# Low parts cut into two or three GpSimd operations, a smaller decode credit in the attention stage, and a last store moved into a branch

## The chip, the cores and the metric

One core of a Trainium2 chip runs the whole program: TensorE (PE) multiplies, VectorE (DVE), ScalarE (ACT) and GpSimd (POOL) do the element work, SyncE (SP) issues nearly all transfers. The metric is device time in microseconds, as the median of several runs.

## The reference

Windowed attention with a linear position bias, then two feed-forward blocks, all on 2 x 768 tokens of width 512:

```python
scores = scale * np.matmul(q, k.transpose(0, 1, 3, 2)) + bias      # 8 heads of 64
a = softmax(where(is_global | is_local, scores, -1e9))             # first 8 keys, last 96 keys
x = a @ v
h = x^T @ U @ V;  u = x + h^T                                      # rank 32, over the tokens
x = u + np.maximum(u @ w_ch1, 0.0) @ w_ch2                         # 512 -> 2048 -> 512
h = np.maximum(x @ w_in, 0.0);  u, v = halves of h                 # 512 -> 2 x 512
v_n = layer norm of v
v_s = np.einsum('ts,bsd->btd', w_spatial, v_n) + b_spatial
out = (u * v_s) @ w_out
```

U, V, w_ch1, w_ch2, w_in and w_out arrive as 64-bit floats; n_global and n_local are data.

## The kernel before

Each large product is done in split precision: an operand a is held as a high part h (a rounded, type fp32r) and a low part l = a - h, and `gemm` (L275 to L277) issues three matmuls per term, h by h, l by h and h by l. Low parts come from `sub` (L58), a subtraction on POOL in most places.

**Weights.** The class `Weights` streams 28 pieces of 128x1024 (six of them 128x768). A coded piece arrives as two halves r (L156, SP). Decoding a half takes an absolute value on ACT (L69) and four DVE operations: clamp (L74), shift (L75) and two joins (L81, L84), each of 128x512. When both halves are done, ACT writes the piece's high part h (L206) and POOL its low part l (L58). A ring holds five pieces. The calls `step(time)` set the pace: each adds a credit, each decode operation spends some. In the attention stage `step(DECODE[0])` is called in four of every six steps after step 24 (the constants MIXING and START); later `step(DECODE[1])` is called once per group of matmuls. The order in which these calls are written is the order on the engines; every engine works through its queue in that order.

**Attention stage** (to about 110 us). Eight head pairs of six query tiles, one step a tile. For each tile PE makes scores sc (L692), DVE adds the bias and takes the row maximum (s and m, L703), ACT exponentiates (e, L706), PE transposes (pt, L716), ACT or DVE copies (et, L63 or L65), PE multiplies by v (xp), DVE normalises every three tiles into x (L755 to L757). There are three banks for sc: PE can start the next scores only when DVE has read the ones two tiles before. After six tiles `mix` adds the rank-32 term: ACT writes xh (L300), POOL xl, PE forms T (L312; ACT L316 and DVE L318 evict it) and u (L291, L295; ACT L339 evicts it), ACT writes uh (L342) and POOL ul. For the last pair DVE makes xl itself.

**Feed-forward stage.** `run` walks four groups g of the hidden width: first products c of token chunk 0 and 1, second product y of chunk 0, then c 2, y 1, y 2. Pieces 0 and 1 are the first products' weights of group 0, pieces 2 and 3 its second products' weights. ACT and DVE evict c (L357, L358), DVE adds y to u (L405). In the rest of the run come the layer norm, the spatial product with gate gs, gh, gl, and twelve output tiles: the last one in two halves, each evicted by ACT (L519) and stored by SP (L520).

**End.** A flag computed on DVE says whether n_local or n_global are out of the windows' reach; each engine loads it (L927) and branches (L928) past a general path that is not taken here.

Of the kernel before, what the change touches and what calls it, by code (L numbers as in the profile page):

```python
# [9 lines left out]
F32 = mybir.dt.float32  # L10
# [7 lines left out]
B, H, S, D = 2, 8, 768, 64  # L18
P = 128
NT = S // P  # L20
DM = H * D
# [27 lines left out]

START, DECODE, MIXING = 24, (1.1, 1.5), (1, 4)
UVSTART = 3
SLOPES = [2.0 ** (-(h + 1)) for h in range(H)]


def sub(eng, out, a, hi):
    eng.tensor_tensor(out=out, in0=a, in1=hi.bitcast(F32), op=ALU.subtract)  # L58


def copy(nc, eng, out, in_):
# [48 lines left out]
class Weights:  # L110
# [86 lines left out]
    def emit(self):  # L197

        nc = self.nc
        for p, (_, _, a, n) in enumerate(self.order):  # L200
            while p >= self.decoded or p - RING >= self.freed:
                yield
            hi = self.ring.tile([P, a, n], F32R, name=f"h{p}", tag="whi")
            lo = self.ring.tile([P, a, n], F32R, name=f"l{p}", tag="wlo")
            wv = self.w32.pop(p)[:, :a * n].rearrange("p (a n) -> p a n", a=a)
            nc.scalar.activation(out=hi, in_=wv, func=AF.Copy)  # L206
            sub(nc.gpsimd, lo, wv, hi)
            self.ready.append((hi, lo))
            yield

# [21 lines left out]
class Moe:  # L232


    def __init__(self, tc, ctx, consts, w, out, ps, pfx):
        self.nc = tc.nc
        self.tc = tc
        self.c = consts
        self.w = w
        self.out = out  # L240
        self.ps = ps
        self.two = self.rest = None
        self.only_scores = False
        self.pfx = pfx
        pool = lambda n, b: ctx.enter_context(tc.tile_pool(name=pfx + n, bufs=b))
        self.act = pool("act", 1)
        self.q = pool("q", 2)
        self.u32 = self.wide("u32")
# [30 lines left out]
    def mix(self, pool, x, b, d, u, last=False):  # L279

        nc, c = self.nc, self.c
        eng = nc.vector if last else nc.gpsimd
        bank = lambda tag: self.two.tile([P, 512], F32, name=self.pfx + "up", tag=tag, bufs=2 if tag == "xp" else 1)

        def transposes(up, hf):
            for t in range(3):  # L290
                nc.tensor.matmul(up[:, t * P:(t + 1) * P], lhsT=x[:, 3 * hf + t], rhs=c["ident"],  # L291
                                 is_transpose=True, start=t == 0, stop=False, skip_group_check=True)

        def by_v(up, hf):
            nc.tensor.matmul(up[:, :HALF], lhsT=T, rhs=c["V"][:, hf * HALF:(hf + 1) * HALF], start=False, stop=True,  # L295
                             skip_group_check=True)

        xh = pool.tile([P, NT, P], F32R, name="xh", tag="xh", bufs=1)
        xl = pool.tile([P, NT, P], F32R, name="xl", tag="xl", bufs=1)
        nc.scalar.activation(out=xh, in_=x, func=AF.Copy)  # L300
        sub(eng, xl, x, xh)
        yield
        ups = [bank("mx")]
        if last:
            ups.append(bank("xp"))
        for hf, up in enumerate(ups):
            transposes(up, hf)
        ap = ups[0][0:3 * RANK, HALF:]
        for hf in range(2):
            for t in range(3 * hf, 3 * hf + 3):  # L310
                for xp in (xh, xl):
                    nc.tensor.matmul(ap, lhsT=c["U"][:, t], rhs=xp[:, t], start=False, stop=False,  # L312
                                     skip_group_check=True)
            yield
        T = pool.tile([P, P], F32R, name="T", tag="T", bufs=1)
        nc.scalar.activation(out=T[0:3 * RANK], in_=ap, func=AF.Copy)  # L316
        hi = slice(2 * RANK, 3 * RANK)
        nc.vector.tensor_tensor(out=T[3 * RANK:], in0=ap[hi], in1=T[hi].bitcast(F32), op=ALU.subtract)  # L318
        yield
        token = lambda hf: slice(b * S + hf * HALF, b * S + (hf + 1) * HALF)  # L320
        if last:
            for hf, up in enumerate(ups):
                by_v(up, hf)
            for hf, up in enumerate(ups):
                sl = token(hf)
                nc.scalar.activation(out=u[0][:, d, sl], in_=up[:, :HALF], func=AF.Copy)  # L326
                nc.vector.tensor_tensor(out=u[1][:, d, sl], in0=up[:, :HALF], in1=u[0][:, d, sl].bitcast(F32),  # L327
                                        op=ALU.subtract)
                yield
                nc.scalar.activation(out=self.u32[:, d, sl], in_=up[:, :HALF], func=AF.Copy)  # L330
            yield
            return
        for hf in range(2):
            if hf:
                ups.append(bank("mx"))
                transposes(ups[1], 1)
            by_v(ups[hf], hf)
            yield
            nc.scalar.activation(out=self.u32[:, d, token(hf)], in_=ups[hf][:, :HALF], func=AF.Copy)  # L339
            yield  # L340
        sl = slice(b * S, b * S + S)
        nc.scalar.activation(out=u[0][:, d, sl], in_=self.u32[:, d, sl], func=AF.Copy)  # L342
        yield
        sub(eng, u[1][:, d, sl], self.u32[:, d, sl], u[0][:, d, sl])
        yield

    def run(self, u, late):

# [160 lines left out]
        wo = w.take(2)  # L509
        for t in range(B * NT):  # L510
            ss = slice(t * P, (t + 1) * P)
            ot = small.tile([P, DM], F32, name="ot", tag="t512", bufs=3)
            parts = 2 if t == B * NT - 1 else 1
            for i in range(parts):
                cs_ = slice(i * DM // parts, (i + 1) * DM // parts)
                op = bank()[:, cs_]
                self.gemm(op, [(gh[:, f, ss], gl[:, f, ss], wo[f // 2][0][:, f % 2, cs_], wo[f // 2][1][:, f % 2, cs_])
                               for f in range(ND)])
                nc.scalar.activation(out=ot[:, cs_], in_=op, func=AF.Copy)  # L519
                nc.sync.dma_start(out=self.out[t // NT, t % NT * P:(t % NT + 1) * P, cs_], in_=ot[:, cs_])  # L520
            if t == B * NT - 1:
                w.free(2)
            yield "g"
# [358 lines left out]
def general_path(tc, w, kq, v, out, nl, ng):  # L882
    nc = tc.nc
    with ExitStack() as ctx:
        cp = ctx.enter_context(tc.tile_pool(name="gconsts", bufs=1))
        ps = ctx.enter_context(tc.tile_pool(name="gps", bufs=2, space=PSUM))
        c = {}
        moe_consts(nc, cp, c)
        c["bsp"] = cp.tile([P, S], F32, name="bsp")
        wt = Weights(tc, ctx, w, "g")  # L890
        moe = Moe(tc, ctx, c, wt, out, ps, "g")
        u = moe.pair("u")
        with ExitStack() as actx:
            moe.two = actx.enter_context(tc.tile_pool(name="gtwo", bufs=1, space=PSUM))
            ap = actx.enter_context(tc.tile_pool(name="gatt", bufs=1))
            moe_const_tiles(ap, c)
            rooms = moe.u32[:, 2:4].rearrange("p d s -> p (d s)")
            for _ in moe_consts2(nc, rooms[:, 0:768].bitcast(I32), rooms[:, 768:1920], w, c):
                pass
            x = ap.tile([P, NT, DM], F32, name="x")  # L900
            for b in range(B):
                with tc.tile_pool(name=f"gatt{b}", bufs=1) as gp:
                    dense_attention(tc, gp, ps, c, b, kq, v, nl, ng, x)
                for d in range(ND):
                    for _ in moe.mix(ap, x[:, :, d * P:(d + 1) * P], b, d, u):
                        pass
        late = late_pools(tc, ctx, "g")
        moe.rest = ctx.enter_context(tc.tile_pool(name="grest", bufs=REST, space=PSUM))
        for _ in moe.run(u, late):
            pass  # L910
# [10 lines left out]
def body(tc, kq, windows, v, ints, w, out):  # L921
    nc = tc.nc
    with ExitStack() as octx:
        keep = octx.enter_context(tc.tile_pool(name="keep", bufs=1))
        with tc.manual_schedule():
            nl, ng, fi = fast(tc, keep, windows, v, ints, w, out)
        general = nc.values_load(fi[0:1, 0:1], min_val=0, max_val=1)  # L927
        with tc.If(general > 0):  # L928
            general_path(tc, w, kq, v, out, nl, ng)


def fast(tc, keep, windows, v, ints, w, out):

    nc = tc.nc
    with ExitStack() as ctx:
# [2 lines left out]
        wt = Weights(tc, ctx, w, "m")  # L938
        c = {"bsp": cp.tile([P, S], F32, name="bsp")}
        moe = Moe(tc, ctx, c, wt, out, ps, "m")  # L940
        u = moe.pair("u")
        actx = ctx.enter_context(ExitStack())
        moe.two = actx.enter_context(tc.tile_pool(name="two", bufs=1, space=PSUM))
# [51 lines left out]
        nc.vector.tensor_copy(fi, flag[:, 3:4])  # L995
        for _ in run:
            wt.step(DECODE[1])
    return nl, ng, fi


# [49 lines left out]
```

## Time and profile before

| | |
|---|---|
| median of 3 runs | 540.03 us (538.39 to 540.51) |
| the profiled execution's own time | 537.04 us |
| its span, first to last instruction | 535.3 us |
| PE busy | 518.6 us, 97% of the span |
| DVE, ACT, POOL busy | 294.1, 204.3, 140.3 us |
| mean granted TensorE clock | 0.993 |

The durations below are from the profiled execution, which lies 3.0 us under the median. PE's busy time counts a matmul in flight, so a stretch of full PE time is one in which PE never waited; it does not say that the clock was full. [...]

### The profile page before, as it was taken

The numbers are of one execution on the slowest core, as the hardware profiler recorded it, in microseconds if no ns is written. First come the engines' busy times: TensorE is split into PE (matmuls) and PEld (weight loads), VectorE is DVE, ScalarE is ACT, GpSimd is POOL, SyncE is SP. The second block draws the span as 40 slices with busy tenths as digits, with TensorE's granted clock in tenths as the row PEclk, the third lists the DMA queues.
The fourth block names the chain that finished last, engine by engine and source line by source line (L and its number), as shares of the span: only waits on it lengthen the run. The fifth ranks groups of instructions, "written<-read, shape, count | busy, mean of one in ns | idle before, by whom it ended". The sixth has DMA issues, their size and how long they took to land.

```text
span 535.3 us, 7195 instructions
## 1 busy us (share of the span) xinstructions
PE 518.6 (97%) x2780; PEld 440.7 (82%) x2780; DVE 294.1 (55%) x655; ACT 204.3 (38%) x380; POOL 140.3 (26%) x91
## 2 busy tenths in 40 slices
PE   7999998899999999999999999999999999999995
PEld 6888876688788888888888888888888889999884
DVE  6877786756697475283831938327275103494300
ACT  4677777564423041131412223034455423222221
POOL 1123314324213120121101121018854412455000
PEclk9999997999999999999999999999999999999999
DMA  8655544211342222022220313103010200100122
GB/s 290 217 216 212 185 136 180 78 43 55 103 143 86 86 80 78 1 83 75 78 80 1 113 46 100 59 0 109 4 56 0 60 29 2 39 1 1 61 99 85
DMA packets 18236, 45.10 MB, mean 84 GB/s; under 512 B 2448, under 2 KB 5136, under 8 KB 17296
## 3 DMA queue, kind: packets, MB, share of 16 engines
q1 hardware_dynamic: 18048, 44.54, 24.6%
q8 instruction: 24, 0.39, 0.3%
q14 instruction: 20, 0.16, 0.1%
q10 hardware_dynamic: 144, 0.00, 0.0%
HBM read 40.99 MB, written 3.15 MB: 82 GB/s over the span
## 4 chain that ended last, share of the span: by engine, by line
PE 91%; DVE 4%; ACT 3%; issue 1%; POOL 0%; POOLq 0%; ACTq 0%; DVEq 0%
PE mmm L276 26%; PE mmm L277 26%; PE mmm L275 25%; PE sc L692 3%; PE pt L716 3%; PE xp L742 2%; PE xp L744 2%; ACT e L706 1%; DVE w L84 1%; DVE s L703 1%; PE mup L312 1%; PE mup L291 1%; PE warm L960 1%; ACT et L63 1%; PE xp L739 1%
## 5 line engine op out<-in xcount | busy, mean ns | idle before, releaser
L58 POOL TENSOR_TENSOR l<-w,h 128x1024 fp32r<-128x1024 f32 (+1 forms) x28 | 64.5, 2305 | 245.3 <-ACT h L206 243.1
L275 PE MATMUL mmm<-uh,h 128*128 128x512 f32 x192 | 75.3, 392 | 0.4 <-ACT uh L326 0.4
L276 PE MATMUL mmm<-ul,h 128*128 128x512 f32 x192 | 74.9, 390 | 0.1
L277 PE MATMUL mmm<-uh,l 128*128 128x512 f32 x192 | 74.8, 390 | 0.0
L275 PE MATMUL mmm<-c,h 128*128 128x512 f32 x192 | 74.7, 389 | 0.0
L276 PE MATMUL mmm<-c,h 128*128 128x512 f32 x192 | 74.7, 389 | 0.0
L277 PE MATMUL mmm<-c,l 128*128 128x512 f32 x192 | 74.7, 389 | 0.0
L358 DVE SCALAR_TENSOR_TENSOR c<-mmm,c 128x512 fp32r<-128x512 f32 x48 | 32.9, 688 | 58.1 <-ACT c L357 58.0
L405 DVE TENSOR_TENSOR u<-u,mmm 128x512 f32<-128x512 f32 x48 | 32.8, 684 | 49.6 <-PE mmm L277 49.6
L357 ACT ACTIVATE c<-mmm 128x512 fp32r<-128x512 f32 x48 | 28.2, 594 | 80.6 <-PE mmm L277 80.5
L69 ACT ACTIVATE w<-r 128x512 f32<-128x512 f32 x44 | 29.3, 668 | 61.0 <-POOL l L58 34.5
L706 ACT ACTIVATE e<-s,m 128x256 f32<-128x256 f32 (+1 forms) x96 | 41.7, 482 | 27.4 <-DVE m L703 27.4
L716 PE MATMUL pt<-ident,e 128*128 128x128 f32 x176 | 46.7, 284 | 0.0
L84 DVE SCALAR_TENSOR_TENSOR w<-r,w 128x512 int32<-128x512 int32 x44 | 42.8, 973 | 0.6
L275 PEld LDWEIGHTS mmm<-uh,h 128*128 128x128 f32 x192 | 36.1, 188 | 8.0 <-ACT uh L326 0.7
L276 PEld LDWEIGHTS mmm<-ul,h 128*128 128x128 f32 x192 | 36.1, 188 | 7.7 <-DVE ul L327 0.4
L276 PEld LDWEIGHTS mmm<-c,h 128*128 128x128 f32 x192 | 36.0, 188 | 7.5
L275 PEld LDWEIGHTS mmm<-c,h 128*128 128x128 f32 x192 | 36.0, 188 | 7.5
L277 PEld LDWEIGHTS mmm<-uh,l 128*128 128x128 f32 x192 | 36.0, 188 | 7.5
L277 PEld LDWEIGHTS mmm<-c,l 128*128 128x128 f32 x192 | 36.0, 188 | 7.4
L206 ACT ACTIVATE h<-w 128x1024 fp32r<-128x1024 f32 (+1 forms) x28 | 28.3, 1009 | 35.9 <-PE mmm L276 32.5
L703 DVE CUSTOM_DVE_ANT_0 s<-sc,bias 128x256 f32<-128x256 f32 (+1 forms) x90 | 33.1, 397 | 7.0 <-ACT e L706 3.7
(127 smaller groups left out, 1018.2 us busy)
## 6 DMA issues: line engine op xcount, KB each, us to landing
r<-in_w_dram SPq DMA_DIRECT2D x32, 512.0 KB, 3.6
kq<-in_windows_dram SPq DMA_DIRECT2D x7, 1024.0 KB, 6.8
vt<-in_v_dram SPq DMA_DIRECT2D x16, 390.0 KB, 4.6
r<-in_w_in_dram SPq DMA_DIRECT2D x8, 512.0 KB, 3.6
out_dram<-ot SPq DMA_DIRECT2D x11, 256.0 KB, 2.0
w<-in_spT_dram SPq DMA_DIRECT2D x6, 384.0 KB, 3.3
r<-in_w_out_dram SPq DMA_DIRECT2D x4, 512.0 KB, 3.6
kq<-in_windows_dram SPq DMA_DIRECT2D x2, 256.0 KB, 4.1
```

What stands on the lines that cost most here:

```text
L58: eng.tensor_tensor(out=out, in0=a, in1=hi.bitcast(F32), op=ALU.subtract)
L69: nc.scalar.activation(out=mag, in_=raw[..., 1].bitcast(F32), func=AF.Abs)
L84: nc.vector.scalar_tensor_tensor(out=oi, in0=raw[..., 0], scalar=29, in1=mi, op0=ALU.logical_shift_right, op1=ALU.bitwise_or)
L206: nc.scalar.activation(out=hi, in_=wv, func=AF.Copy)
L275: self.nc.tensor.matmul(out, lhsT=lh, rhs=rh, start=first and i == 0, stop=False)
L276: self.nc.tensor.matmul(out, lhsT=lh, rhs=rl, start=False, stop=False)
L277: self.nc.tensor.matmul(out, lhsT=ll, rhs=rh, start=False, stop=last and i == n - 1)
L358: nc.vector.scalar_tensor_tensor(out=cc[:, 1, f], in0=cp, scalar=0.0, in1=cc[:, 0, f].bitcast(F32), op0=ALU.max, op1=ALU.subtract)
L405: nc.vector.tensor_tensor(out=u32[:, d, tok], in0=u32[:, d, tok], in1=yp, op=ALU.add)
L703: nc.vector.tensor_tensor_reduce(out=s[:, :n], in0=sps[hd], in1=bs, scale=-0.125, scalar=3e38, op0=ALU.add, op1=ALU.min, accum_out=m)
L706: nc.scalar.activation(out=e[:, :n], in_=s[:, :n], func=AF.Exp, bias=m, scale=-1.0)
L716: nc.tensor.transpose(pt[:, k * P:(k + 1) * P], es[hd][:, j * P:(j + 1) * P], c["ident"])
```

## The change

A new helper cuts a subtraction along the second axis into equal parts, issued one after the other. It is used for the low parts of weight pieces (two parts of 128x512, or of 128x384), for xl and for ul (three parts of 128x256 each); for the last pair's xl DVE runs the three parts. The credit of a decode step in the attention stage goes from 1.1 to 0.9. The last output tile gets a buffer of its own in the outermost pool, and the store of its second half is no longer issued behind its eviction but in an `Else` of the branch, which is the side taken here. In the general path the same tile's halves are stored as before.

```diff
-START, DECODE, MIXING = 24, (1.1, 1.5), (1, 4)
+START, DECODE, MIXING = 24, (0.9, 1.5), (1, 4)
...
+def sub_parts(eng, out, a, hi, n):
+
+    m = a.shape[1] // n
+    for i in range(n):
+        part = slice(i * m, (i + 1) * m)
+        sub(eng, out[:, part], a[:, part], hi[:, part])
...
             nc.scalar.activation(out=hi, in_=wv, func=AF.Copy)
-            sub(nc.gpsimd, lo, wv, hi)
+            sub_parts(nc.gpsimd, lo, wv, hi, 2)
...
-        sub(eng, xl, x, xh)
+        sub_parts(eng, xl, x, xh, 3)
...
-        sub(eng, u[1][:, d, sl], self.u32[:, d, sl], u[0][:, d, sl])
+        sub_parts(eng, u[1][:, d, sl], self.u32[:, d, sl], u[0][:, d, sl], 3)
         yield
+
+    def store(self, t, cols_, ot):
+        self.nc.sync.dma_start(out=self.out[t // NT, t % NT * P:(t % NT + 1) * P, cols_], in_=ot[:, cols_])
+
+    def store_end(self):
+
+        self.store(B * NT - 1, slice(DM // 2, DM), self.end)
...
-            ot = small.tile([P, DM], F32, name="ot", tag="t512", bufs=3)
-            parts = 2 if t == B * NT - 1 else 1
+            end = t == B * NT - 1
+            parts = 2 if end else 1
+            if end and self.end is not None:
+                ot = self.end
+            else:
+                ot = small.tile([P, DM], F32, name="ot", tag="t512", bufs=3)
...
-                nc.sync.dma_start(out=self.out[t // NT, t % NT * P:(t % NT + 1) * P, cs_], in_=ot[:, cs_])
+                if i < parts - 1 or ot is not self.end:
+                    self.store(t, cs_, ot)
...
-        with tc.If(general > 0):
+        with tc.If(general > 0) as choice:
             general_path(tc, w, kq, v, out, nl, ng)
+        with choice.Else():
+
+            store_end()
```

The smaller credit moves decode operations. On DVE, in the second part of the sixth head pair (from the x of its first three tiles to the copy and the next s), the program before has one join behind x and, behind the copy, a join, a clamp and a shift (L81 and L84 are the joins, L74 the clamp, L75 the shift):

```order
L757 TENSOR_TENSOR x<-xp,r 128x2x3x64
L81 SCALAR_TENSOR_TENSOR w_1130<-r_928,w_1130 128x512
L703 ISA s,m<-sc,bias 128x256
...
L65 COPY et<-pt 128x256
L84 SCALAR_TENSOR_TENSOR w_1130<-r_928,w_1130 128x512
L74 TENSOR_SCALAR w_1130<-w_1130 128x512
L75 TENSOR_SCALAR w_1130<-w_1130 128x512
L703 ISA s,m<-sc,bias 128x256
```

The same place in the changed program (L89 and L92 are the joins there, L82 the clamp, L83 the shift, L724 is s, L73 the copy):

```order
L778 TENSOR_TENSOR x<-xp,r 128x2x3x64
L92 SCALAR_TENSOR_TENSOR w_1031<-r_937,w_1031 128x512
L82 TENSOR_SCALAR w_1175<-w_1175 128x512
L83 TENSOR_SCALAR w_1175<-w_1175 128x512
L724 ISA s,m<-sc,bias 128x256
...
L73 COPY et<-pt 128x256
L89 SCALAR_TENSOR_TENSOR w_1175<-r_939,w_1175 128x512
L724 ISA s,m<-sc,bias 128x256
```

Two operations moved from behind the copy to behind x, and the decode stands two and more operations further back.

On ACT, where the first evictions of chunk 1's c stand (h_1844 is the high part of piece 3, h_1908 of piece 4), before:

```order
L206 ACTIVATE h_1844<-w_1545 128x1024
L316 ACTIVATE T<-mup 96x128
L326 ACTIVATE uh<-mup 128x384
...
L330 ACTIVATE u_79<-mup 128x384
L357 ACTIVATE c<-mmm 128x512
L69 ACTIVATE w_1871<-r_1867 128x512
L357 ACTIVATE c<-mmm 128x512
L206 ACTIVATE h_1908<-w_1757 128x1024
```

And now (h_1915 is the high part of piece 3; L214 writes h, L373 evicts c):

```order
L325 ACTIVATE T<-mup 96x128
L335 ACTIVATE uh<-mup 128x384
...
L339 ACTIVATE u_79<-mup 128x384
L373 ACTIVATE c<-mmm 128x512
L214 ACTIVATE h_1915<-w_1708 128x1024
```

Piece 3's high part moved from ahead of T to behind the first eviction of that chunk. From piece 7 on the order is nearly as before.

On SP, at the end of the program before:

```order
L520 DMA out_dram<-ot 128x256 [waits DMAHW7_49,Activation_49]
L520 DMA out_dram<-ot 128x256 [waits DMAHW0_49,Activation_49]
L928 COMPARE_AND_BRANCH
```

And now, where the side taken stands behind the general path:

```order
L357 DMA out_dram<-end 128x256 [waits DMAHW7_49,Activation_49]
L949 COMPARE_AND_BRANCH
...
L357 DMA out_dram<-end 128x256 [waits DMAHW0_49,Activation_49]
L949 UNCONDITIONAL_BRANCH [waits DMAHW1_49,DMAHW2_49,DMAHW3_49,DMAHW4_49,DMAHW5_49,DMAHW6_49,DMAHW7_49]
```

The second half's store moved from ahead of the branch to behind it.

## Rows read from the trace of the kernel before

**Rows 1.** Windows: from:to, length, PE, PEld, DVE, ACT, POOL busy, clock, DMA, GB/s.

```profile
80.00:90.00 10.00, 7.71 (x53) 5.85 (x53) 7.87 (x25) 6.91 (x15) 4.15 (x2) 0.85 0.56 204
90.00:100.00 10.00, 10.00 (x79) 9.10 (x78) 5.64 (x22) 6.53 (x15) 2.23 (x2) 0.81 0.30 104
...
150.00:160.00 10.00, 10.00 (x46) 8.29 (x45) 9.68 (x18) 2.83 (x4) 0.00 (x0) 1.00 0.52 167
```

**Rows 2.** PE timeline, 60 to 112: start, length, instruction [wait before it <- releaser].

```profile
67.75 1.13 PE L692 MATMUL sc<-kq 64*128 64x256 f32 x6 [1.27 <-DVE m L703]
72.53 1.13 PE L692 MATMUL sc<-kq 64*128 64x256 f32 x6 [0.50 <-DVE m L703]
87.49 2.07 PE L692 MATMUL sc<-kq 64*128 64x256 f32 x6 [2.29 <-DVE m L703]
105.47 1.13 PE L692 MATMUL sc<-kq 64*128 64x256 f32 x6 [2.31 <-DVE m L703]
110.51 0.55 PE L291 MATMUL mup<-ident,x 128*128 128x128 f32 x3 [1.28 <-ACT u L339]
```

**Rows 3.** DVE timeline, decode operations and the s behind them.

```profile
65.16 2.18 DVE L81 SCALAR_TENSOR_TENSOR w<-r,w 128x512 int32<-128x512 int32 x1
70.65 0.68 DVE L84 SCALAR_TENSOR_TENSOR w<-r,w 128x512 int32<-128x512 int32 x1
...
84.34 1.95 DVE L84 SCALAR_TENSOR_TENSOR w<-r,w 128x512 int32<-128x512 int32 x1
86.22 0.41 DVE L74 TENSOR_SCALAR w<-w 128x512 f32<-128x512 f32 x1
86.67 0.43 DVE L75 TENSOR_SCALAR w<-w 128x512 int32<-128x512 int32 x1
87.01 0.42 DVE L703 CUSTOM_DVE_ANT_0 s<-sc,bias 128x256 f32<-128x256 f32 x1
```

**Rows 4.** POOL timeline, low parts of four sizes and places.

```profile
64.86 1.94 POOL L58 TENSOR_TENSOR ul<-u,uh 128x768 fp32r<-128x768 f32 x1 [3.83 <-ACT uh L342]
81.60 2.37 POOL L58 TENSOR_TENSOR l<-w,h 128x1024 fp32r<-128x1024 f32 x1 [4.62 <-ACT h L206]
83.91 1.83 POOL L58 TENSOR_TENSOR ul<-u,uh 128x768 fp32r<-128x768 f32 x1
389.39 1.29 POOL L58 TENSOR_TENSOR v<-hv,v 128x512 fp32r<-128x512 f32 x1 [1.03 <-ACT v L431]
```

**Rows 5.** Timeline of the gate stage, POOL and DVE at the same time.

```profile
470.41 2.73 POOL L58 TENSOR_TENSOR gl<-gs,gh 128x384 fp32r<-128x384 f32 x2 [4.16 <-ACT gh L482]
470.75 1.51 DVE L84 SCALAR_TENSOR_TENSOR w<-r,w 128x512 int32<-128x512 int32 x1
```

**Rows 6.** ACT timeline around the fourth wait of PE.

```profile
102.58 0.66 ACT L69 ACTIVATE w<-r 128x512 f32<-128x512 f32 x1
...
105.51 0.91 ACT L706 ACTIVATE e<-s,m 128x256 f32<-128x256 f32 x2 [2.27 <-DVE m L703]
```

**Rows 7.** ACT timeline, then PE timeline, where the first second product begins.

```profile
141.53 0.59 ACT L357 ACTIVATE c<-mmm 128x512 fp32r<-128x512 f32 x1
...
144.45 1.05 ACT L206 ACTIVATE h<-w 128x1024 fp32r<-128x1024 f32 x1
...
143.73 0.39 PE L277 MATMUL mmm<-c,l 128*128 128x512 f32 x1
...
144.41 0.39 PE L277 MATMUL mmm<-c,l 128*128 128x512 f32 x1
```

**Rows 8.** The last stores on SP, SP's wait at the branch, stores' time to landing.

```profile
528.55 0.33 SPq L520 DMA_DIRECT2D out_dram<-ot  x1
...
529.94 0.33 SPq L520 DMA_DIRECT2D out_dram<-ot  x1
...
SPq L928 <- SPq L928: 3.0, 1, 3.0
...
out_dram<-ot SPq DMA_DIRECT2D x2, 128.0 KB, 2.4
```

More of the change, by code (lines that the diff above doesn't have):

```diff
@@ L243, in __init__ @@
         self.only_scores = False
+        self.end = None
         self.pfx = pfx
@@ L925, in body @@
         with tc.manual_schedule():
-            nl, ng, fi = fast(tc, keep, windows, v, ints, w, out)
+            nl, ng, fi, store_end = fast(tc, keep, windows, v, ints, w, out)
         general = nc.values_load(fi[0:1, 0:1], min_val=0, max_val=1)
-        with tc.If(general > 0):
+        with tc.If(general > 0) as choice:
             general_path(tc, w, kq, v, out, nl, ng)
+        with choice.Else():
+            store_end()
 def fast(tc, keep, windows, v, ints, w, out):
@@ L940, in fast @@
         moe = Moe(tc, ctx, c, wt, out, ps, "m")
+        moe.end = keep.tile([P, DM], F32, name="end")
         u = moe.pair("u")
@@ L997, in fast @@
             wt.step(DECODE[1])
-    return nl, ng, fi
+    return nl, ng, fi, moe.store_end
 def kernel(**inputs):
```

## The prediction

> **What bounds the kernel now.** I read the windows first. From 145 us to the end PE is full at full clock: one of those windows stands in [rows 1], and nothing that DVE, ACT or POOL do there shows in the time as long as it stays so. The change can only pay where PE is not full, and that is the attention stage from 60 to 112 us. [...] At full clock the same matmuls would have taken 10 x (0.15 + 0.19) = 3.4 us less. Next the PE timeline, for the waits themselves: five, of 1.27, 0.50, 2.29, 2.31 and 1.28 us, together 7.65 [rows 2]. Four are scores that wait for m, so for DVE having read the earlier scores; the fifth waits for ACT's u. Last the DVE and POOL timelines at those times, for why DVE was late. A join takes 0.68 us where it is alone (70.65), but 2.18 and 1.95 at 65.16 and 84.34 [rows 3]. POOL was then in a ul of 128x768: from 64.86 to 66.80, and from 83.91 to 85.74 [rows 4]. The join ended about half a microsecond after the ul each time, so it stood still until POOL's instruction was over. Of the 11.05 us lost (7.65 and 3.4), this and the decode ahead of s are the cause of most.
>
> **First wait (1.27).** Nothing moves here; ul is cut in three. POOL takes 1.29 us for 512 columns and 2.37 for 1024 [rows 4], so 0.54 per 256 and an estimated 0.75 for a part of 256. The first part ends at 64.86 + 0.75 = 65.61, the join 0.5 later at 66.1 instead of 67.3. Gain 1.2; bounds 0 (below) and 1.27.
>
> Whether DVE gets in between two parts is the condition, and there is a row for it: two gl of POOL ran directly behind each other, 2.73 us for both, and a join that began at 470.75, in the first, took 1.51 [rows 5]. It ended at 472.26; had it waited for both gl (to 473.14) it could not have. So DVE is let in at the seam, and POOL's second operation then waits for DVE.
>
> **Second wait (0.50).** The clamp and the shift that stood ahead of this s now stand behind the next x: 0.41 + 0.43 us [rows 3] leave DVE's path, more than the wait. Gain 0.5; bounds 0.3 and 1.1, since DVE was behind for longer than PE stood.
>
> **Third wait (2.29).** Behind the copy stood a join, a clamp and a shift, 84.34 to 87.01 = 2.67 us [rows 3]; now one join, 0.68, stands there, and l is no longer ahead of ul in POOL's queue, so that ul is over by then. s comes 2.0 us sooner by this. Against it, two operations more, 0.84 us, stand behind x, and the third of them meets the ul there and waits for a part, up to 0.75. Of that 1.6 I take 0.65, as ACT, which has its long h (1.05) after this slot and not in it, makes up the rest. Net gain 1.35; bounds 0.4 and 2.0.
>
> **The low clock (3.4).** The clock fell at the third wait, 2.29 us long. The scores after the first, second and fourth, at 1.13 us, show that it did not fall there [rows 2]. With 0.9 us left of the third I take it that it stays up: 3.4. Bounds 0 and 3.4; the fourth wait, just as long, did not bring it down, so length alone doesn't tell.
>
> **Fourth and fifth wait (2.31, 1.28).** The same slot one pair later: now only a clamp and a shift stand behind the copy, and POOL is idle. s comes 1.95 sooner. But ACT has now h and an absolute value between the two pairs of e: from 102.6 on, 1.05 [rows 7] and 0.66 [rows 6], so its e come at 104.3 instead of 105.51, 1.2 to 1.3 sooner and not 1.95. PE catches up with ACT at the fifth wait and stands 0.65 longer there. Gain of both 1.3; bounds 0.8 and 2.6.
>
> Together 1.2 + 0.5 + 1.35 + 3.4 + 1.3 = 7.75 us.
>
> **What it costs: piece 3 comes late.** In group 0 the second product's first matmul with l of piece 3 stands at 143.73, and the first that reads its second half at 144.41 [rows 7]. Before, ACT wrote that piece's h ahead of the last T. Now it writes it behind the first eviction of c, 141.53 to 142.1 [rows 7], so from 142.1 to 143.1; PE's first matmul with h is two before 143.73, at 143.28: in time. l begins at 143.1 to 143.3. Two parts of 1.29 end at 144.5 and 145.8, and a wait of DVE's operation in the seam (clamp and shift of piece 4 stand there, 0.4 each) puts the second at 146.2. PE stands until 146.2 where it would have begun at 144.41: 1.8 us, in two waits. Bounds 0.7 (all parts alone, started at once, h a little sooner) and 2.6. [...]
>
> **Smaller.** l of piece 2 now runs where DVE clamps, shifts and makes the last xl: xl up to 0.9 late, of which PE's other work covers most; 0.2, bounds 0 and 0.9. The cut itself costs POOL 0.2 us per piece (2 x 1.29 against 2.37) and 0.4 per xl or ul; from 145 us on it lies under full PE, and would cost only if POOL became the last to arrive, which its 140 us of 535 make unlikely: 0. The ring fills again by piece 7, so later stages keep their order.
>
> **The store.** Before, SP issues the last store at 529.94 and goes on 3.0 us after its branch; the transfer lands within 2.4 us, inside that wait [rows 8]. Now SP can branch behind the first half's store, 528.55 + 0.33, and goes on at 531.9, 1.4 us sooner. The store issues then and lands up to 2.4 later, 534.3, and only the last of SP's closing work lies behind it, where before all 2.0 us of that followed 533.3. I take 0.3 us later; bounds 1.4 sooner and 1.3 later. [...]
>
> **Sum.** 7.75 - 1.8 - 0.2 - 0.3 = 5.45 us. The profiled execution goes from 537.04 to 531.6. Its distance to the median, 2.99, I carry over: 540.03 - 5.45 = 534.6.
>
> **Rivals.**
> - *Low clock remains.* [...] For it: the third and fourth wait were equally long and only one brought the clock down. Against: no wait over 2 us is left. 534.6 + 3.4 = 538.0. Chance 0.16.
> - *More is gained.* Piece 3 arrives in time (1.8 back), third wait at its upper bound (0.65), store free (0.3): 531.8; lower still, to 530, if the runs, which lie above the profile, had more low clock to lose. Chance 0.18.
> - *The cut does not do what it says.* POOL runs its parts through, and DVE waits for all: ul then lasts 2.2 us. First wait -0.4, second 0.5, third 0.4, clock 0, fourth and fifth 1.3, costs 1.8: 540.0. Against it the join at 470.75. Chance 0.08.
> - *Slower: piece 3 becomes the bound.* If its decode begins only behind the second ul of the last mix, at 141.0 (because its raw halves or ACT come late), it needs twice 0.41 + 0.43 + 2 x 0.68 = 4.4, h 1.05, l 2.6: 149.05. PE would stand from 143.28 on, 5.8 us, and the clock would fall, 3.4 more. 7.75 - 0.5 - 9.2 = -1.95: 542.0. With the clock falling, it decides from a wait of 3.85 us. Against it: three of the second half's four operations stand ahead of that ul. Chance 0.06.
> - The forecast: 0.52.
>
> **Numbers.** About 0.5%, 2.7 us, is what a measurement can tell from no change. Under 537.3 lie the forecast, "more", and a part of the low clock case: 0.73. Within 0.5% lie most of that case, the cut without effect and half of the slower one: 0.23. Slower: 0.04. The range 530.0 to 538.6 leaves out the last two rivals (0.14) and a little below.
>
> **What would show it.** Right: no join over 1.4 us beside POOL in 60 to 110; waits of sc for m under 1.2 us each; granted clock 1.00 from 10 us to the end; two waits of PE for POOL's l, together near 1.8 us, about 137 us; end of the span within 6 us of PE's last matmul as now. Wrong: joins of 2 us beside the cut ul; a low window anywhere; a wait of several us for ACT's h at the second product; SP standing for its last store for over 2 us.

## The result and the profile after

| | before | after |
|---|---|---|
| median of the executions measured together | 539.21 us (537.88 to 540.51) | 531.54 us (531.23 to 531.99) |
| ratio, 95% interval | | 0.9866 (0.9844 to 0.9889) |
| the profiled execution | 537.04 | 531.99 |
| its span | 535.3 | 530.2 |
| POOL, DVE busy | 140.3, 294.1 | 155.0, 293.8 |

The change takes 7.67 us off the median (1.3%), and 5.05 off the profiled execution. The forecast was 534.6, in a range of 530.0 to 538.6. Ratios leave out executions more than 1.5% above the fastest of their kernel, here and below: one of 1024.35 us of the cut alone, which its median leaves out too, and the three longest of the kernel with a whole ul.

In the changed program the lines are shifted: scores sc are L713, s and m L724, the clamp L82, the shift L83, the joins L89 and L92, u L348, weights' h L214, the matmuls of `gemm` L284 to L286, the end L1071. The windows of the changed kernel (columns as in [rows 1]: from and to, length, busy time of PE, PEld, DVE, ACT and POOL, granted clock, DMA share, GB/s):

```profile
80.00:90.00 10.00, 9.96 (x83) 8.43 (x84) 8.36 (x31) 8.81 (x19) 6.12 (x7) 1.00 0.52 178
90.00:100.00 10.00, 9.82 (x80) 8.07 (x78) 8.14 (x33) 8.18 (x18) 5.22 (x5) 1.00 0.17 55
100.00:110.00 10.00, 8.68 (x62) 7.62 (x61) 4.19 (x11) 4.95 (x12) 2.67 (x5) 1.00 0.15 54
130.00:140.00 10.00, 8.36 (x34) 5.60 (x33) 9.05 (x19) 6.58 (x12) 2.77 (x2) 1.00 0.16 53
```

The clock is at 1.00 where [rows 1] had 0.85 and 0.81, and PE is nearly full from 80 to 100. There are two weak windows: 100 to 110, where the fifth wait is left, and 130 to 140, where piece 3 comes late. What PE waited for, in all (engine, line, for what: total, times, longest):

```profile
PE mup L300 <- ACT u L348: 1.8, 3, 1.3
PE mmm L286 <- POOL l L58: 1.1, 2, 0.7
...
PE sc L713 <- DVE m L724: 0.2, 1, 0.2
```

Of the four waits of scores for m in [rows 2] one is left, of 0.2 us; shorter ones are not listed, and the eight scores at 79.28 show that there are such. On PE's timeline:

```profile
66.37 1.13 PE L713 MATMUL sc<-kq 64*128 64x256 f32 x6 [0.19 <-DVE m L724]
...
79.28 1.89 PE L713 MATMUL sc<-kq 64*128 64x256 f32 x8
...
102.59 0.55 PE L300 MATMUL mup<-ident,x 128*128 128x128 f32 x3 [1.32 <-ACT u L348]
...
133.95 0.41 PE L284 MATMUL mmm<-c,h 128*128 128x512 f32 x1
...
135.63 0.40 PE L285 MATMUL mmm<-c,h 128*128 128x512 f32 x1
136.72 0.50 PE L286 MATMUL mmm<-c,l 128*128 128x512 f32 x1 [0.69 <-POOL l L58]
...
138.15 0.50 PE L286 MATMUL mmm<-c,l 128*128 128x512 f32 x1 [0.46 <-POOL l L58]
...
523.08 0.28 PE L286 MATMUL mmm<-h,gl 128*128 128x256 f32 x1
```

The same places before, for the eight scores, for the first matmul of the first second product, and for the last matmul:

```profile
80.91 1.13 PE L692 MATMUL sc<-kq 64*128 64x256 f32 x8
...
141.91 0.40 PE L275 MATMUL mmm<-c,h 128*128 128x512 f32 x1
...
529.22 0.28 PE L277 MATMUL mmm<-h,gl 128*128 128x256 f32 x1
```

The join that took 2.18 us in [rows 3], and a shift that the new order puts beside the next ul, on DVE's timeline:

```profile
64.87 1.10 DVE L89 SCALAR_TENSOR_TENSOR w<-r,w 128x512 int32<-128x512 int32 x1
...
78.80 0.84 DVE L83 TENSOR_SCALAR w<-w 128x512 int32<-128x512 int32 x1
79.56 0.41 DVE L724 CUSTOM_DVE_ANT_0 s<-sc,bias 128x256 f32<-128x256 f32 x1
...
82.95 0.68 DVE L89 SCALAR_TENSOR_TENSOR w<-r,w 128x512 int32<-128x512 int32 x1
83.55 0.42 DVE L724 CUSTOM_DVE_ANT_0 s<-sc,bias 128x256 f32<-128x256 f32 x1
```

POOL's ul beside the first of them lasts longer than the one in [rows 4], 2.67 us for three parts against 1.94 for one operation, and nobody waits for it:

```profile
64.57 2.67 POOL L58 TENSOR_TENSOR ul<-u,uh 128x256 fp32r<-128x256 f32 x3 [3.54 <-ACT uh L351]
```

At the end SP now waits twice: at the branch, as in [rows 8], and for the store that it issues behind it:

```profile
SPq L1071 <- DMA out_dram<-end: 2.6, 1, 2.6
SPq L1071 <- SPq L1071: 2.5, 1, 2.5
```

### The profile page after: what moved, and what is told of

It reads as the page before. It is cut to its first block, busy times and chain, and to the rows that moved or that the text cites. A ratio compares the mean times of both kernels' runs of the same rounds, so it can differ in the third digit from the quotient of the medians.

```text
span 530.2 us, 7263 instructions
## 1 busy us (share of the span) xinstructions
PE 516.2 (97%) x2780; PEld 437.8 (83%) x2780; DVE 293.8 (55%) x657; ACT 203.8 (38%) x380; POOL 155.0 (29%) x147
## 4 chain that ended last, share of the span: by engine, by line
PE 88%; DVE 4%; ACT 3%; DMA 2%; issue 1%; SPq 1%; POOL 1%; ACTq 0%; DVEq 0%
PE mmm L286 25%; PE mmm L284 25%; PE mmm L285 25%; PE sc L713 3%; PE pt L737 2%; PE xp L763 2%; PE xp L765 2%; DMA kq<-in_windows_dram 2%; ACT e L727 2%; DVE s L724 1%; PE mup L321 1%; PE mup L300 1%; ACT et L71 1%; POOL l L58 1%; DVE w L89 0%
## 5 line engine op out<-in xcount | busy, mean ns | idle before, releaser
L58 POOL TENSOR_TENSOR l<-w,h 128x512 fp32r<-128x512 f32 (+1 forms) x56 | 73.4, 1332 | 223.5 <-ACT h L214 214.5
L286 PE MATMUL mmm<-c,l 128*128 128x512 f32 x192 | 74.9, 390 | 1.1 <-POOL l L58 1.1
L284 PE MATMUL mmm<-uh,h 128*128 128x512 f32 x192 | 75.3, 392 | 0.4 <-ACT uh L335 0.4
L286 PE MATMUL mmm<-uh,l 128*128 128x512 f32 x192 | 74.8, 390 | 0.0
L284 PE MATMUL mmm<-c,h 128*128 128x512 f32 x192 | 74.8, 389 | 0.0
L373 ACT ACTIVATE c<-mmm 128x512 fp32r<-128x512 f32 x48 | 28.3, 596 | 76.5 <-PE mmm L286 76.5
L286 PEld LDWEIGHTS mmm<-c,l 128*128 128x128 f32 x192 | 36.0, 188 | 9.5 <-POOL l L58 2.0
L214 ACT ACTIVATE h<-w 128x1024 fp32r<-128x1024 f32 (+1 forms) x28 | 28.2, 1008 | 40.1 <-PE mmm L285 35.0
L284 PEld LDWEIGHTS mmm<-uh,h 128*128 128x128 f32 x192 | 36.1, 188 | 8.0 <-ACT uh L335 0.7
L284 PEld LDWEIGHTS mmm<-c,h 128*128 128x128 f32 x192 | 36.0, 188 | 7.8 <-ACT h L214 0.2
L286 PEld LDWEIGHTS mmm<-uh,l 128*128 128x128 f32 x192 | 36.0, 188 | 7.5
L89 DVE SCALAR_TENSOR_TENSOR w<-r,w 128x512 int32<-128x512 int32 x44 | 37.9, 860 | 0.7
L724 DVE CUSTOM_DVE_ANT_0 s<-sc,bias 128x256 f32<-128x256 f32 (+1 forms) x90 | 32.9, 396 | 7.5 <-ACT e L727 4.3
```

The costliest lines, as they stand in the source:

```text
L89: nc.vector.scalar_tensor_tensor(out=mi, in0=raw[..., 1], scalar=-0x40000000, in1=mi, op0=ALU.bitwise_and, op1=ALU.bitwise_or)
L284: self.nc.tensor.matmul(out, lhsT=lh, rhs=rh, start=first and i == 0, stop=False)
L286: self.nc.tensor.matmul(out, lhsT=ll, rhs=rh, start=False, stop=last and i == n - 1)
L373: nc.scalar.activation(out=cc[:, 0, f], in_=cp, func=AF.Relu)
L724: nc.vector.tensor_tensor_reduce(out=s[:, :n], in0=sps[hd], in1=bs, scale=-0.125, scalar=3e38, op0=ALU.add, op1=ALU.min, accum_out=m)
```

## The experiments

The reasons under test: the cut lets DVE in at the seams, the smaller credit takes decode operations off the path of s, the clock then stays up, piece 3 costs 1.8 us, and the store costs something. The kernels were measured in three groups. Ratios are against the kernel before in the same group; its median was 537.69 us in the first, 538.74 in the second and 538.60 in the third.

### One part at a time, and the store

The first kernel is the kernel before with the cut alone:

```diff
-            sub(nc.gpsimd, lo, wv, hi)
+            sub_parts(nc.gpsimd, lo, wv, hi, 2)
-        sub(eng, xl, x, xh)
+        sub_parts(eng, xl, x, xh, 3)
-        sub(eng, u[1][:, d, sl], self.u32[:, d, sl], u[0][:, d, sl])
+        sub_parts(eng, u[1][:, d, sl], self.u32[:, d, sl], u[0][:, d, sl], 3)
```

> The kernel before with only GpSimd's low parts cut (l in 2, xl and ul in 3); the decode rate 1.1 and the old last store stay. Theory (DVE is let in at the seams; the decode rate does the rest): the first wait falls from 1.27 to about 0.2 us, the third from 2.29 to about 1.4 (its join no longer stands behind a whole ul), the second and fourth stay at 0.5 and 2.3, piece 3 is on time (no wait of PE for l). Time 2 us below before if the clock still falls (537 against 539.2), 5 us below if the third wait was what brought it down. Rival (the cut does nothing by itself, all comes from the decode rate): joins beside POOL stay near 2 us, time within 0.5 us of before.

Measured: 535.34 us, ratio 0.9949 (0.9919 to 0.9980), so the rival without any gain falls. The first wait went, as expected. The third did not shrink at all, and the scores behind it ran at low clock (six take 2.07; the windows show 0.79 from 80 to 90 us and 0.87 from 90 to 100). PE's timeline:

```profile
66.12 1.13 PE L700 MATMUL sc<-kq 64*128 64x256 f32 x6 [0.18 <-DVE m L711]
...
86.01 2.07 PE L700 MATMUL sc<-kq 64*128 64x256 f32 x6 [2.38 <-DVE m L711]
...
104.08 1.13 PE L700 MATMUL sc<-kq 64*128 64x256 f32 x6 [2.29 <-DVE m L711]
```

DVE's timeline ahead of the third wait says why:

```profile
82.89 1.00 DVE L92 SCALAR_TENSOR_TENSOR w<-r,w 128x512 int32<-128x512 int32 x1
83.81 0.94 DVE L82 TENSOR_SCALAR w<-w 128x512 f32<-128x512 f32 x1
84.79 0.83 DVE L83 TENSOR_SCALAR w<-w 128x512 int32<-128x512 int32 x1
```

Three operations meet the three parts of ul (82.60 to 85.33) and each is slowed: 1.00 + 0.94 + 0.83 = 2.77 us. In [rows 3] the same three took 1.95 + 0.41 + 0.43 = 2.79: the first stood for the whole ul, the others ran alone. Here cutting spread the delay over the row, and s, which stands behind the third operation, gained nothing. So the expectation of 1.4 us here was wrong, and so was any hope of the cut by itself where a row of decode stands ahead of s.

The second kernel has the credit alone:

```diff
-START, DECODE, MIXING = 24, (1.1, 1.5), (1, 4)
+START, DECODE, MIXING = 24, (0.9, 1.5), (1, 4)
```

> The kernel before with only the decode rate 0.9; low parts uncut, old last store. Theory: the first wait stays (1.27), the second goes, the third falls to about 1 us, the fourth goes, the clock stays up (3.4 us), and piece 3's uncut l makes PE wait about 1.2 to 1.9 us in one piece near 140 us. Time 4 to 5 us below before, about 534.7. Rival (the cut is what shortens the third wait): third wait still about 2 us, clock falls, time 1 us below before or less, 538 or more.

Measured: 540.90 us, ratio 1.0055 (1.0022 to 1.0089), slower than before. The waits of PE in the attention stage came out as expected, the one at 101 us apart, which I had taken to go:

```profile
67.06 1.13 PE L692 MATMUL sc<-kq 64*128 64x256 f32 x6 [1.26 <-DVE m L703]
...
84.01 1.13 PE L692 MATMUL sc<-kq 64*128 64x256 f32 x6 [1.14 <-DVE m L703]
...
101.05 1.13 PE L692 MATMUL sc<-kq 64*128 64x256 f32 x6 [1.20 <-DVE m L703]
...
147.40 0.50 PE L277 MATMUL mmm<-c,l 128*128 128x512 f32 x1 [1.77 <-POOL l L58]
```

Behind each of the first three stands one DVE operation that met a whole ul of POOL:

```profile
64.48 2.18 DVE L81 SCALAR_TENSOR_TENSOR w<-r,w 128x512 int32<-128x512 int32 x1
...
81.70 1.92 DVE L75 TENSOR_SCALAR w<-w 128x512 int32<-128x512 int32 x1
...
98.33 2.32 DVE L84 SCALAR_TENSOR_TENSOR w<-r,w 128x512 int32<-128x512 int32 x1
```

In the changed kernel, with the same order on DVE, these took 1.10, 0.84 and 0.81. What I had not expected is the clock. The windows of this kernel:

```profile
60.00:70.00 10.00, 8.74 (x70) 7.43 (x70) 7.09 (x22) 6.32 (x15) 2.29 (x2) 0.91 0.23 89
70.00:80.00 10.00, 10.00 (x72) 8.39 (x71) 6.63 (x27) 6.91 (x16) 1.83 (x1) 0.75 0.70 237
80.00:90.00 10.00, 8.86 (x58) 7.68 (x58) 7.54 (x23) 6.45 (x13) 3.78 (x2) 0.76 0.25 74
90.00:100.00 10.00, 9.85 (x81) 8.09 (x79) 7.86 (x22) 6.26 (x14) 4.18 (x3) 0.90 0.39 115
100.00:110.00 10.00, 8.95 (x49) 7.42 (x49) 6.98 (x26) 7.02 (x15) 4.15 (x3) 0.66 0.16 53
```

The clock column falls short of 1.00 by 10 x (0.09 + 0.25 + 0.24 + 0.10 + 0.34) = 10.2 us in all, three times the 3.4 of [rows 1], although no wait there is longer than 1.26. So the third wait's 2.29 us was not what had to go. The theory had the waits nearly right and the time wrong by 6 us; the rival had a time on the right side for a wrong reason, since the third wait did shrink.

The other two kernels concern the store. One is the changed kernel with the old store, the other the kernel before with only the store moved:

```diff
-        with tc.If(general > 0) as choice:
+        with tc.If(general > 0):
             general_path(tc, w, kq, v, out, nl, ng)
-        with choice.Else():
-            store_end()
```

> The changed kernel with the end half tile's store put back ahead of the branch. Theory (the store behind the branch leaves its landing uncovered): the tail after PE's last matmul goes from 6.8 back to 5.8 us, all else is as in the changed kernel, so 1.1 us less than its 531.5: 530.4. Rival (the longer tail came from something else, the branch's own time or the Else block): no difference, 531.5.

> The kernel before with only the end half tile's store moved into the branch that skips the general path. Theory: tail 6.8 instead of 5.8 us, so 1.1 us slower than before, 540.3 against 539.2, attention unchanged with its five waits and the low clock. Rival: the store's place costs nothing by itself, within 0.3 us of before.

Measured: 530.77 us, 0.9873 (0.9822 to 0.9925), and 538.99 us, 1.0008 (0.9980 to 1.0037) with a median 1.3 over that of before. The times agree with a cost of about 1 us but cannot settle it. The tails do: from the end of PE's last matmul to the end of the span it is 5.35 to 5.76 us in the ten profiles with the old store, and 6.12 to 7.12 in the four with the new one, 1.16 more by the means. In the kernel with only the store moved the landing shows as its own wait:

```profile
SPq L1071 <- DMA out_dram<-end: 2.9, 1, 2.9
```

with the old store in the otherwise changed kernel only the branch is left:

```profile
SPq L949 <- SPq L949: 2.5, 1, 2.5
```

The comparison was repeated in the third group:

> The changed kernel with the old last store once more, beside the changed kernel itself on the same chip. Theory (the store behind the branch leaves 1.1 to 1.2 us of its landing uncovered): 1.1 below the changed kernel. Rival (it is noise of single profiles): no difference.

> The changed kernel itself, for the comparison with the three others of this call: 531.3, tail after PE's last matmul 6.7.

Measured: 531.68 and 532.28 us (529.71 to 532.91, and 531.90 to 533.20), tails 5.35 and 6.12. The sign is the same, the size within the scatter of these runs.

### Which cut, and which credit

All four belong to the second group; the three behind the changed kernel have the old store.

> The changed kernel again, beside the three below. Expected 531.5, as measured, with the clock up throughout, so that its executions lie within about 1 us.

Measured: 531.10 us (530.20 to 532.27), ratio 0.9847 (0.9821 to 0.9873), mean granted clock 0.996 to 0.999 in the four executions.

```diff
-        sub_parts(eng, u[1][:, d, sl], self.u32[:, d, sl], u[0][:, d, sl], 3)
+        sub(eng, u[1][:, d, sl], self.u32[:, d, sl], u[0][:, d, sl])
```

> The changed kernel with the old last store and only ul in one operation of 768 columns again (l in two, xl in three, decode rate 0.9). Theory (a DVE operation that meets a whole ul stands 1.9 to 2.3 us, and it is this that PE waits for): three waits of about 1.2 us at 66, 83 and 100 us as with all parts whole, piece 3 at 1.15; the clock falls in most executions. 530.8 + 3.2 of waits = 534 where the clock stays up, and 537 to 540 by the median with low stretches. Rival (the cut of l or xl did it): attention as in the changed kernel, 531.

Measured: ten executions from 533.45 to 542.90, median 538.97 (535.04 of the seven that the ratio takes), ratio 0.9969 (0.9931 to 1.0007). Two of the three waits came back, and the clock fell behind the first (0.89 from 60 to 70 us, 0.77 from 70 to 80, then 1.00 to 120 us). PE's timeline:

```profile
67.29 1.59 PE L713 MATMUL sc<-kq 64*128 64x256 f32 x6 [1.26 <-DVE m L724]
...
84.26 1.13 PE L713 MATMUL sc<-kq 64*128 64x256 f32 x6 [1.15 <-DVE m L724]
```

The third did not: that ul (96.27 to 98.42) met no more than the end of a join (96.06, 0.69 us). The cut of ul is thus most of what the cut is worth: without it four fifths of the gain are gone by the two ratios (0.0031 is left of 0.0153).

```diff
-            sub_parts(nc.gpsimd, lo, wv, hi, 2)
+            sub(nc.gpsimd, lo, wv, hi)
```

> The changed kernel with the old last store and only the weights' l in one operation of 1024 columns again (ul and xl in three). Theory (l meets no DVE operation ahead of an s at rate 0.9): attention as in the changed kernel, waits under 0.4 but for the one of 1.3 on ACT's u, clock up; piece 3's l makes PE wait once, about 1.8 us as with all parts whole, in place of 1.15 in two. 530.8 + 0.6 = 531.4. Rival (seams let DVE in and make l late, so whole is sooner): the wait for l is below 1.15 and the time below 530.8.

Measured: 533.97 us, 0.9909 (0.9881 to 0.9937), 2.6 over the expectation. Piece 3 was as expected (one wait of 1.77), but neither theory had the rest: in the attention stage a join took 2.11 us beside a whole l (POOL, 84.10 to 86.47) where it takes 1.01 beside the halves, and PE waited 0.41 for an m and 1.84 for the fifth wait's u; the windows show a clock of 0.83 from 100 to 110 us. The cut of l matters in the attention stage, not only at piece 3. No kernel has xl alone whole, so what its cut is worth was not tested.

```diff
-START, DECODE, MIXING = 24, (0.9, 1.5), (1, 4)
+START, DECODE, MIXING = 24, (1.0, 1.5), (1, 4)
```

> The changed kernel with the old last store and the decode rate 1.0 in place of 0.9. In this order ACT writes piece 3's h as early as in the kernel before, so the wait for its l (1.15) should go; but two joins in a row stand ahead of s in the slots of 66 and 83 us where one stood. Theory (what counts is how many DVE operations stand ahead of s beside POOL): waits of about 1 us come back at one or two of these places and the clock falls in some executions, time 531 to 535. Rival (with the parts cut the order doesn't matter): waits as with 0.9, time 1.1 below the changed kernel with the old store, about 529.7, and the best of all.

Measured: 536.52 us, 0.9960 (0.9940 to 0.9981): 5.4 over the changed kernel of the same group, which has the new store, and a little worse than the theory had it. Piece 3 was in time and cost nothing, but on PE's timeline

```profile
85.94 1.13 PE L713 MATMUL sc<-kq 64*128 64x256 f32 x6 [1.92 <-DVE m L724]
...
103.97 0.55 PE L300 MATMUL mup<-ident,x 128*128 128x128 f32 x3 [2.25 <-ACT u L348]
```

two joins of 1.13 and 1.10 us beside the parts of one ul stand ahead of the first of them. With every part cut, the order still decides.

### Making piece 3 early again

```diff
-                wt.step(DECODE[0])
+                wt.step(DECODE[0] if i < 46 else 1.5)
```

> The changed kernel with the old last store, and the decode rate 1.5 in place of 0.9 from slot 46 on (the last slots, behind the last score that waits). Up to slot 45 nothing moves. Theory: ACT writes piece 3's h before the last T as in the kernel before, so PE's 1.15 of waiting for its l goes; up to 0.5 of it comes back where five DVE operations and a third ACT operation now stand ahead of the last T and x. 0.6 to 1.1 below the changed kernel with the old store, so about 529.8. Rival (the decode ahead of x and T delays PE as much): a wait for xl, T or uh of about 1 us takes its place, no difference.

Measured: 528.66 us (528.03 to 528.68), 0.9813 (0.9784 to 0.9841): the best of all, and 3.0 below the same kernel without the edit in the same group, where 0.6 to 1.1 was expected. What PE waited for:

```profile
PE mup L300 <- ACT u L348: 1.8, 3, 1.3
...
PE mmm L284 <- ACT uh L335: 0.4, 1, 0.4
PE sc L713 <- DVE m L724: 0.2, 1, 0.2
```

The wait for l is gone and none took its place. In the two profiles the spans differ by 1.7 us (526.2 and 527.9), and so does the stretch from the first second product to PE's end (387.6 and 389.4). So piece 3 gives back all of its 1.8, and not the 1.15 that its two waits add up to, by which the expectation went. The other 1.3 of the medians is hardly the clock, which is 0.997 or more in both; the kernel without the edit scatters over 3.2 us in that group, and why is open.

```diff
+        done = len(self.ready)
         next(self.work, 0)
+        time += self.held
+        self.held = time if done == 1 and len(self.ready) > done else 0.0
+        if self.held:
+            return
         self.credit = min(self.credit, 0.0) + time
```

> As the kernel with rate 1.5 from slot 46 on, and in the one slot of the last pair in which ACT writes piece 1's h (1.04 us), the decode step (ACT's absolute value, 0.66, and DVE's clamp and shift) is held back to the next slot. Theory (the wait of 1.32 on u comes from the 1.7 us of h and absolute value between two pairs of e on ACT): it falls to about 0.7, time 0.6 lower. Rival (ACT is only the next to last, and the four DVE operations that now stand in a row behind x are later): a wait for m takes its place, no gain or a loss of about 1.

Measured: 531.98 us, 0.9885 (0.9855 to 0.9915), 3.3 worse than the kernel without it. The rival won, and by more than it had said, though the wait stands on u and not on m: the fifth wait grew to 3.16 us. DVE's timeline:

```profile
97.12 1.31 DVE L82 TENSOR_SCALAR w<-w 128x512 f32<-128x512 f32 x1
98.46 1.38 DVE L83 TENSOR_SCALAR w<-w 128x512 int32<-128x512 int32 x1
99.87 1.22 DVE L89 SCALAR_TENSOR_TENSOR w<-r,w 128x512 int32<-128x512 int32 x1
```

Three operations that take 0.42 + 0.43 + 0.68 = 1.5 us alone took 3.9 beside the parts of l and xl, all of it ahead of s, and the windows show a clock of 0.83 from 100 to 110 us. Whether a shorter stay of ACT alone would shorten the fifth wait was therefore not tested.

## Why the prediction was right, point by point

| term | forecast | in the two profiles |
|---|---|---|
| first wait | 1.2 | 1.08 |
| second wait | 0.5 | 0.80, less 0.54 for u behind it: 0.26 |
| third wait | 1.35 | 2.57, less 0.76 at the scores of the tile before: 1.81 |
| fourth and fifth | 1.3 | 2.40, less 0.47 at the scores of the tile before and 0.44 for u: 1.49 |
| low clock | 3.4 | 2.97 |
| elsewhere in the stage | 0 | 0.06 |
| attention stage | 7.75 | 7.67 |
| piece 3 | -1.8 | -1.82 |
| xl of the last pair | -0.2 | no wait |
| store | -0.3 | -1.07 |
| start of the program | 0 | 0.29 |
| sum | 5.45 | 5.07 |
| distance of the profile to the median | 2.99 in both | 2.17 before, -0.45 after |

The attention stage is taken from the start of the first wait to the first matmul of the first second product: 66.48 to 141.91 before, 66.19 to 133.95 after, 75.43 and 67.76 us. Piece 3 is the stretch from there to the end of PE's last matmul, 387.59 and 389.41. PE has the same matmuls in the same order in both kernels, so each term of the stage is the time between the starts of the same two matmuls, before less after. The first wait, for one, is read from the first scores of its tile to the first xp behind them: 65.78 to 68.80 before, 65.49 to 67.43 after, 3.02 and 1.94. This also counts what the timeline shows as a shorter wait or as none.

**The mechanism held.** DVE is let in at the seam of two parts, as the two gl had said [rows 4, 5]: a join 1.10 us in place of 2.18, a shift 0.84 where the same order with a whole ul gives 1.92. The join beside the whole ul ends at 67.34, about half a microsecond behind the ul's 66.80 [rows 3, 4]; the one beside the three parts ends at 65.97 and does not wait for their end at 67.24. With three DVE operations in a row cutting changed which of them pays, not the sum: 2.77 against 2.79 us. POOL's ul took 2.67 against 1.94. That is why the two edits need each other: on their medians the cut alone gives 2.4, the credit alone costs 3.2, and both with the old store give 6.9.

**The terms of the attention stage came out near their sizes.** The low clock gave 2.97 us, not the 3.4 by which the two windows of [rows 1], 0.85 and 0.81, fall short of 1.00. The six scores behind the third wait took 2.00 us to the xp behind them, and the six behind the first 1.05: 0.95 more. From the xp behind them to the next scores PE took 4.68 us (89.49 to 94.17), where the same work took 2.64 one head pair earlier at a clock of 1.00 (73.59 to 76.23) and 2.66 in the changed kernel. Before, on PE's timeline:

```profile
73.59 0.44 PE L739 MATMUL xp<-vt,et 128*128 128x65 f32 x2
...
76.23 0.93 PE L692 MATMUL sc<-kq 64*128 64x128 f32 x8
...
89.49 0.69 PE L739 MATMUL xp<-vt,et 128*128 128x65 f32 x2
...
94.17 0.93 PE L692 MATMUL sc<-kq 64*128 64x128 f32 x8
```

The step that was a little off is the pricing of the whole low stretch at half its length. By windows of 0.1 us in the profile of before the clock goes from 1.00 to 0.50 at 87.0 to 87.1, nearly half a microsecond before the third wait ended, and there PE stood anyway; it is back at 1.00 at 93.9, and 0.50 between. A stretch can cost far less than half its length, as the kernel with only the store moved shows. It has the order of before in this stage; its windows show 0.97, 0.69, 0.99, 0.84, 0.85 and 0.98 from 60 to 120 us, 10 x 0.68 = 6.8 us short of 1.00 and so twice the 3.4 of [rows 1], yet its first second product comes only 0.7 us later, counted from the first wait, and its second and fifth wait are gone.

The third wait went altogether, and gave 2.57 us where the working had 2.0. The 0.65 charged for the two operations behind x were due, and came to 0.76: the eight scores there take 1.89 us for 1.13. The fifth wait stayed (1.28, now 1.32) rather than growing by 0.65, but 0.87 was lost ahead of it, at scores and at a u. The errors of these terms have both signs, and that their sum is met within 0.1 us is luck.

**Piece 3 cost what was forecast, 1.82,** though the two waits on PE's timeline add up to only 1.15. The rest lies around them: from 135.63 to 136.72 PE took 1.09 us for a step of 0.23, and the matmul behind a wait takes 0.50 for 0.40. The kernels in which piece 3 is in time (before, the cut alone, credit 1.0, the late higher credit) all need 387.6 to 387.7 us from there to PE's end, the ones with a cut l that is late 389.4, the ones with a whole l that is late 389.7 to 389.8. So the price of 1.8, which has the delay in the seam in it, was right in size. The delay itself was smaller than its 0.4: the two parts took 2.77 us (135.32 to 138.09) for 2 x 1.29 alone, and l began at the late end of the range, 1.37 us behind the first matmul of the second product.

**The store was the term that was wrong inside the profile:** 1.07 us, within its bounds, not 0.3. Counted from the end of PE's last matmul (529.50 before, 523.36 after), SP is through the branch at 3.83 before and at 1.95 after, so 1.9 sooner, more than the 1.4 of the working. The store is issued at 2.10 (525.46). But it lands 3.4 us behind its issue and not 2.4, the duration of [rows 8] that I had used (the middle of two stores of 3.0 and 1.9), and 1.3 of closing work stands behind that: 2.10 + 3.42 + 1.31 = 6.83, where the tail before was 5.76. The term that failed is the landing, by 1.0 us. The forecast had named "SP standing for its last store for over 2 us" as a sign against it, and it came.

**What failed in the number is the step from profile to median.** I carried over 2.99 us as if it belonged to the measurement. A fourth execution made it 2.17 before, and after it is -0.45. It seems to belong mostly to the kernel. Over the 55 executions of the kernel before that ran beside the experiments, the mean granted clock went from 0.977 to 0.993, and the profile on which the sum was made was one of the best (0.993). By the clock, their medians are 535.8 us at 0.990 and more (4 executions), 537.8 at 0.985 to 0.989 (33), 538.6 at 0.982 to 0.984 (7) and 539.8 below (11). The clock is not all of it: the 33 alone run from 536.6 to 540.8. The twelve executions of the changed kernel lie at 0.996 to 0.999, and in its profile what is missing lies behind PE's last matmul (1.00 from 10 us to there, 0.69 behind). So the typical execution before (median clock 0.986) had about twice the low time of its profile (1 - 0.986 against 1 - 0.993), and the change took it. This is the case "more is gained" of the forecast (531.8), by the half of it that spoke of more low clock to lose; its other half, piece 3 in time and a free store, did not happen. That the measured 531.5 lies so near to 531.8 is luck. That the clock makes the difference between executions rests on this ordering and on the windows of the experiments; no run changed the clock by itself.

## What to carry to other kernels

Cutting an operation of POOL let DVE in between here, but only a single DVE operation beside it gained (1.10 us for 2.18); a row of three beside the same work took as long as before (2.77 us for 2.79). So cut and reorder together, and count how many DVE operations stand ahead of the one that PE waits for. Short waits can come with a low clock: in the kernel with the credit alone, three of about 1.2 us stood beside granted clocks of 0.66 to 0.91 in the windows from 60 to 110 us, and it took 10.1 us more than the kernel that adds the cut, with the old store in both (540.90 and 530.77). And the profile of one execution may show the mildest case: look at the clock of all executions before a sum is carried to the median. Where two kernels give PE the same matmuls in the same order, compare the starts of matmuls rather than the waits.

## What was not expected of the hardware

- The length of a wait did not tell here whether the clock falls behind it. It fell in stretches that held waits of 1.26, 1.14 and 1.20 us (the credit alone, 0.66 to 0.91), and not in the profile of the changed kernel, whose longest wait in the stage is 1.32 (1.00 in every window from 60 to 120 us); in [rows 2] it fell at a wait of 2.29 and not at one of 2.31. The same order of work gave one low stretch in the profile of before (0.85 and 0.81 from 80 to 100 us) and more than one in that of the kernel with only the store moved (0.69 from 70 to 80 us, 0.99 from 80 to 90, 0.84 and 0.85 from 90 to 110).
- Waits on PE's timeline were shorter than what they cost: 1.15 us of waits for 1.82 us of time at piece 3, and 0.76 us at the scores of 79.28 with no wait listed.
- The store behind the branch paid both the branch (a wait of 2.5 us) and its landing (waits of 1.9 to 2.9 us); with the store ahead of the branch only the branch's wait is left (2.5 to 3.0 us), and the tail is 1.16 us shorter by the means.
